# Linear attention and MLP, two layers: M as three float32r products, late parts of q behind it, and a new order in the first tile

## The chip, the cores and the metric

The kernel runs on one core of a Trainium2 chip. The time is the device time of one execution in microseconds, the median of several runs. Lower is better. A profile of one execution gives what each engine did: TensorE (PE, its weight loads PEld), VectorE (DVE), ScalarE (ACT), GpSimd (POOL) and SyncE (SP, which here issues transfers). "fp32r" is the type in which TensorE multiplies float32 data with one pass; the kernel gets its accuracy back by splitting an operand into a high part (rounded to fp32r) and a low part (the residual), and adding three products: high·high, low·high, high·low.

## The reference

Two layers, each with two halves, over x of 2048 rows and 640 columns; 32 heads of 20 columns:

```python
q, k, v = split(layernorm(x) @ wqkv)          # per head, S x 20
pq, pk = phi(q), phi(k)                       # where(t>0, t+1, exp(t)) + 1e-6
kv = einsum("bhsd,bhse->bhde", pk, v)         # 20 x 20 for each head
z  = einsum("bhsd->bhd", pk)
o  = (pq @ kv) / (pq . z + 1e-6)
x  = x + o @ wo                               # half A
h  = relu(layernorm(x) @ w1 + b1) ** 2
x  = x + h @ w2 + b2                          # half B
```

The kernel never forms v. With xh the normed rows, it accumulates G = xhᵀ·phi(k) over all rows, then kv = Gᵀ·wv restricted to the heads' diagonal blocks (a mask), and then M = kv·wo, a 640 x 640 matrix. So half A's output is (phi(q) divided by its denominator) @ M.

## The kernel before

All rows are cut into 16 tiles of 128. The instructions are laid out by hand: each engine runs them in the order in which the code issues them, and the 8 PSUM banks are assigned by number. SP issues transfers in order too.

**Half A, tile by tile.** A tile is normed, transposed (xT, high and low), and multiplied with the split weights kq into k and q (`part`, line 419 in the profile, three products for each of five blocks of 128). ACT takes the exponential from PSUM (`Phi.exp`, L519), DVE does the rest of phi (`Phi.rest`, L526 and L527). k goes to kh (high on ACT, low on DVE), POOL adds it to acc for the denominators (L727), and TensorE adds to G, whose five blocks stay in banks 3 to 7 (`g_part`). Columns 512 to 639 of phi(k) go to GT by `gt_part`, summed into SBUF by DVE (L557). q is stored to DRAM. For some tiles, those in LATE, q is not computed there: its halves of 320 columns wait as late parts, 15 matmuls each (`late_q`), to be run where TensorE would stand still.

**The first tile of layer 0** has an order of its own (L569 to L601 and L766). The weights arrive as raw blocks; ACT copies each to its high part (`first_loads.high`, L205), DVE makes the residual (`first_loads.low`, L211). ACT copies the transposed x out of two PSUM banks to xT's high part (L587), DVE makes its low part (L591). ACT's order before: high parts of the first and the second weight block, then the two copies of xT. TensorE then runs products 0 and 1 of each block and, LAG = 2 blocks later, product 2 (`first_part`).

**The stage around M**, once a layer, after the last tile. In the order of the code: late parts beside the split of acc and the denominators zbc; the last tile's G blocks, copied out of PSUM by ACT (L920); the last GT sums (L557); one late part (`late_q(1)`); five transposes of GT into banks 1 and 2 and their copy Gs (L929); the split of tile 0's divided q, pT (`b_split`, L148 and L149). Then six times `kv_make`: five (or ten) float32 matmuls (L957) into one of the banks 3 to 7 and 2, and DVE's multiplication by the mask into kvbd (L961). Between them DVE runs steps of tile 1's division (`b_step`, L651 to L672), spread by KV_STEPS. Then six times `m_make`, in the order M_ORDER: two float32 matmuls of 320 columns, kvbd by wo (L970), into two banks, from which ACT copies to Mc (L977) and stores it to DRAM; the last two blocks are also copied directly to Mr (L993). SP reads the stored rows in another arrangement into Mr (L999, `m_read`). Then four late parts (three by `late_q(Q[0])`, one more), the splits of Mr into uM (`m_split`, L1028 and L1029), and the projection `proj` of the first tiles (L440). Lists like `side_work` hold small moves of DVE that are run at given points.

wo comes into SBUF in the last tiles of half A by `load_vo`, on SP, as raw float32 rows. The rows of x for the residual sum of tiles 0 and 1 (`b_load_x`) are loaded within the loop over `kv_make`.

**Half B** (L1182, L1200 to L1205, L1242) is the MLP, with prepared weights; the change leaves it alone.

Of the kernel before, what the change touches and what calls it, by code (L numbers as in the profile page):

```python
# [65 lines left out]
OUT0 = (fast(4), fast(9))  # L66
STAY = 1
FB0 = 0
KV_STEPS = (0, 1, 1, 1, 1, 0)


M_ORDER = (0, 1, 2, 3, 5, 4)
# [18 lines left out]
def kernel(  # L91
# [382 lines left out]
    for layer in range(N_LAYERS):  # L474
        src = [rows(t, xf) for t in range(NT)] if layer == 0 else x2
        last_layer = layer == N_LAYERS - 1

        md = dram.tile([D, D], F32, name=f"md_{layer}", tag="md")
        pqd = [dram.tile([P, D], F32, name=f"pq_{layer}_{t}", tag=f"pq_{t}") for t in range(NT)]
# [79 lines left out]
        if layer == 0:  # L559

            psw = bank(3)

            def warm(n):
                for _ in range(n):
                    nc.tensor.transpose(psw[:, :P], ident, ident)

            warm(N_WARM)
            a_load(0, src)
            first_loads.step(0, 5)  # L569
            a_load(1, src)  # L570
            a_stats(0, add=nc.vector)
            first_loads.high(2)

            mv, rs = sts.pop(("a", 0))
            T4[0] = tmp.tile([P, TG, 2, D], R32, tag="T", name="xT", bufs=2)
            xT[0] = chunks(T4[0][:, 0])
            runs = [(bank(4), 0, 2), (bank(5), 2, DC)]
            for ps, a, b in runs:
                v = xt[0][:, a * P : b * P]
                nc.vector.tensor_scalar(v, v, mv[:, 0:1], rs, op0=ALU.subtract, op1=ALU.mult)  # L580
            for ps, a, b in runs:
                for c in range(a, b):
                    nc.tensor.transpose(
                        ps[:, (c - a) * P : (c - a + 1) * P], xt[0][:, c * P : (c + 1) * P], ident
                    )
                d = T4[0][:, 0, 0, a * P : b * P]
                nc.scalar.activation(d, ps[:, : (b - a) * P], AF.Copy)  # L587
            first_loads.low(1)
            for ps, a, b in runs:
                d = T4[0][:, 0, :, a * P : b * P]  # L590
                nc.vector.tensor_tensor(  # L591
                    out=d[:, 1], in0=ps[:, : (b - a) * P], in1=d[:, 0].bitcast(F32), op=ALU.subtract
                )
            first_loads.low(1)
            first_loads.step(2, 5)
            a_stats(1)
            first_loads.step(2, 5)
            a_apply(1)
            a_load(2, src)
            first_loads.step(1, 5)  # L600
            first_loads.high(1)  # L601
            first_loads.low(1)
# [15 lines left out]

        def load_vo(i):

            u = utile("uraw").bitcast(F32).rearrange("p (j n) -> p j n", j=2)
            for j in range(2):
                c = 2 * (i % 3) + j
                if i < 3 and c < DC:
                    nc.sync.dma_start(u[:, j], wqkv[c * P : (c + 1) * P, 2 * D :])
                if i >= 3:
                    n = head_rows(c)
                    nc.sync.dma_start(u[:n, j], wo[c * HR : c * HR + n, :])
                vo["v" if i < 3 else "o", c] = u[:, j]

        pq, xr, pT, yzp, yzx, xn = {}, {}, {}, {}, {}, {}
        dens, xTb = {}, {}
# [59 lines left out]
        def b_out(t, ps):  # L692
            proj(ps, pT.pop(t), M)
# [48 lines left out]
        for t in range(NT):  # L742
# [5 lines left out]
            if layer == 0:  # L748
                prep.store()
                if 6 <= t < 6 + 2 * DC:  # L750
                    keep_kq(*divmod(t - 6, 2))
            if t >= 13:
                b_load_pq(t - 13)
                load_vo(2 * t - 26)
                load_vo(2 * t - 25)
            if first:
# [15 lines left out]
                seq = [(nm, c) for nm in "kq" for c in range(DC)]  # L772
                for n in range(len(seq) + LAG):
                    if n < len(seq):
                        first_part(*seq[n], (0, 1))
                    if n >= LAG:
                        first_part(*seq[n - LAG], (2,))
                    if n == DC + LAG - 1:
                        for j in range(2):
                            fk.exp(j * HD, pss["k"][j][:, :HD])  # L780
                    if n == AT_T:
                        first_loads.high(2)
                        a_trans(1, bank(4, 2))
# [137 lines left out]
        for j in range(2):  # L921
            gt_part(NT // 2 - 1, j, xbank())
        b_blocks(0)
        late_q(1)

        psT = bank(1, 2)
        transpose5(psT, GT_)
# [12 lines left out]

        b_split(0, xtile("pT"))

        u = xtile("kvbd", F32).rearrange("p j n -> p (j n)")
        kvbd = [u[:, HR * c : HR * (c + 1)] for c in range(NH)]
        maskf = mask.rearrange("p h d -> p (h d)")
        kvb = [3, 4, 5, 6, 7, 2]

        def kv_make(c):
            n = head_rows(c)
            kvb.append(kvb.pop(0))  # L950
            ps = bank(kvb[-1])

            o, m = HR * c, max(min(DM - HR * c, n), 0)
            parts = [v for v in ((0, m, G, o), (m, n, Gs, max(o - DM, 0))) if v[0] < v[1]]
            for q0, q1, g, w0 in parts:
                for d in range(DC):
                    nc.tensor.matmul(  # L957
                        ps[:n, q0:q1], vo["v", d][:, o : o + n],
                        g[:, d, w0 : w0 + q1 - q0], start=d == 0, stop=d == DC - 1,
                    )  # L960
            nc.vector.tensor_tensor(out=kvbd[c][:n, :n], in0=ps[:n, :n], in1=maskf[:n, :n], op=ALU.mult)  # L961

        mb = [4, 2, 6]

        def m_make(c):
            mb.append(mb.pop(0))
            ps = bank(mb[-1], 2)
            n, o = head_rows(c), HR * c
            for j in range(2):
                nc.tensor.matmul(  # L970
                    ps[:n, j * 512 : j * 512 + HD], kvbd[c][:n, :n],
                    vo["o", c][:n, j * HD : (j + 1) * HD], start=True, stop=True,
                )

            if c not in M_NEAR:
                u = ftile("Mc")
# [56 lines left out]
        for c in range(NH):  # L1033
            kv_make(c)
            if c == 0:
                b_load_pq(3)
            if c == 1:
                b_load_x(0)
            if c == 3:
                b_load_x(1)  # L1040
            if KV_STEPS[c]:
                b_step(1, KV_STEPS[c])
        side_work.append(lambda: b_split(1, xtile("pT")))
        run_side(1)
        sg.close()
        sm = ExitStack()
        mp = sm.enter_context(
# [8 lines left out]
        for i, c in enumerate(M_ORDER):  # L1056
            m_make(c)
            b_step(2)
            for r in M_READ.get(c, ()):
                m_read(*r)  # L1060
            if i > 4:
                run_side(1)
            if i > 0:
                b_step(3)
        side_work.append(lambda: b_split(3, xtile("pT")))
        late_q(Q[0])
        for m in range(3):
            m_split(m)
        run_side(1)
        late_q(1)  # L1070
        m_split(3)
        m_split(4)
        m_sum(4)
# [604 lines left out]
```

## Time and profile before

| | before |
|---|---|
| median of 3 runs | 1342.88 us (1342.48 to 1343.03) |
| the profiled execution | 1345.11 us |
| its span in the trace | 1343.2 us |
| PE busy | 1336.0 us, 99% |
| DVE busy | 891.5 us, 66% |
| ACT busy | 697.8 us, 52% |
| POOL busy | 124.2 us, 9% |

The profiled execution is 2.2 us longer than the median, and its span covers all but 1.9 us of it. In the rows of a timeline stand the start (us from the span's start), the busy time, engine, line, operation, output and inputs, shapes, and the number of instructions that the row puts together; in square brackets stands the time the engine was idle before, and what released it. In rows of groups three durations stand as shortest, median and longest in ns, then the first and the last start.

### The profile page before, as it was taken

What the parts mean: (1) busy time and instruction counts of PE and PEld (TensorE: products, weight loads), DVE (VectorE), ACT (ScalarE), POOL (GpSimd) and SP (SyncE); (2) the same over time, 40 slices, a digit from 0 to 9 for tenths busy, and PEclk for the clock granted to TensorE, in tenths of its full rate; (3) what the DMA queues carried; (4) which work ended last, traced back from release to release, by engine and by line L of the source; (5) the groups of instructions that cost most, each with busy time, mean ns of one, the idle gap of its engine ahead of it and who ended that gap; (6) DMA issues with size and microseconds to landing.
All of it is one profiled execution on the core that took longest, in us unless ns stands there. A gap on an engine that the chain in (4) does not pass through costs nothing.

```text
span 1343.2 us, 18730 instructions
## 1 busy us (share of the span) xinstructions
PE 1336.0 (99%) x6746; PEld 1154.6 (86%) x6746; DVE 891.5 (66%) x1601; ACT 697.8 (52%) x1612; POOL 124.2 (9%) x171
## 2 busy tenths in 40 slices
PE   9999999999999999999999999999999999999998
PEld 8888999988888888888888899998888888888887
DVE  7888868877766756533367678678777567665323
ACT  4887844634545426424547686355434535454131
POOL 2222310000000000000012132100000000000000
PEclk9999999999999999999999999999999999999999
DMA  6787846575557475588521115176547565564654
GB/s 206 246 293 263 284 125 197 176 282 172 189 207 225 137 265 175 168 296 300 207 99 44 55 40 145 52 243 253 159 150 277 161 204 189 206 221 139 247 169 154
DMA packets 100638, 255.88 MB, mean 191 GB/s; under 512 B 12787, under 2 KB 37747, under 8 KB 99907
## 3 DMA queue, kind: packets, MB, share of 16 engines
q1 hardware_dynamic: 99322, 252.04, 55.6%
q10 hardware_dynamic: 1224, 2.65, 0.7%
q8 instruction: 53, 0.87, 0.3%
q14 instruction: 39, 0.31, 0.1%
HBM read 195.96 MB, written 58.49 MB: 189 GB/s over the span
## 4 chain that ended last, share of the span: by engine, by line
PE 99%; DMA 0%; ACT 0%; SPq 0%; DVE 0%; DVEq 0%; issue 0%
PE PS L419 38%; PE PS L1242 28%; PE PS L1182 28%; PE PS L440 3%; PE PS L970 1%; PE PS L957 1%; PE PS L766 1%; DMA st<-in_A_wqkv_dram 0%; PE PS L388 0%; PE PS L907 0%; PE PS L1282 0%; ACT kq L205 0%; DVE x L1293 0%; SPq L227 0%; SPq L457 0%; DVEq L1673 0%
## 5 line engine op out<-in xcount | busy, mean ns | idle before, releaser
L1182 PE MATMUL PS<-xTb,u 128*128 128x512 f32 x1400 | 332.8, 390 | 0.0
L407 ACT ACTIVATE z<-y 32x160 f32<-32x160 f32 x880 | 294.0, 334 | 59.3 <-DVE y L394 49.4
L1182 PEld LDWEIGHTS PS<-xTb,u 128*128 128x128 f32 x1400 | 262.4, 188 | 53.6
L419 PE MATMUL PS<-kq,xT 128*128 128x320 f32 (+2 forms) x1575 | 283.4, 335 | 0.0
L1242 PE MATMUL PS<-u,h 128*128 128x512 f32 x1120 | 279.6, 390 | 0.0
L419 PEld LDWEIGHTS PS<-kq,xT 128*128 128x128 f32 x1575 | 250.3, 188 | 26.7 <-DVE rl L527 0.5
L1200 ACT ACTIVATE hr<-PS,b1sb 128x512 f32<-128x512 f32 x104 | 71.4, 687 | 348.3 <-PE PS L1182 346.9
L1242 PEld LDWEIGHTS PS<-u,h 128*128 128x128 f32 x1120 | 208.1, 188 | 39.5
L1204 DVE TENSOR_TENSOR hr<-hr 128x512 f32<-128x512 f32 x104 | 71.3, 685 | 148.2 <-ACT h L1201 148.2
L419 PE MATMUL PS<-kh,xh 128*128 128x512 f32 x480 | 124.2, 392 | 0.0
L519 ACT ACTIVATE e<-PS 128x320 f32<-128x320 f32 (+4 forms) x128 | 53.4, 435 | 108.7 <-PE PS L419 99.1
L378 POOL TENSOR_SCALAR rs<-mv 128x1 f32<-128x1 f32 x63 | 28.8, 458 | 860.4 <-DVE mv L376 860.4
L419 PEld LDWEIGHTS PS<-kh,xh 128*128 128x128 f32 x480 | 87.2, 188 | 15.2 <-DVE kh L730 0.4
L526 DVE TENSOR_SCALAR e<-e 128x320 f32<-128x320 f32 (+4 forms) x128 | 41.6, 325 | 66.3 <-ACT e L519 66.3
L1242 PE MATMUL PS<-h,u 128*128 128x512 f32 x280 | 79.1, 391 | 0.0
L1205 DVE TENSOR_TENSOR h<-hr,h 128x512 fp32r<-128x512 f32 x104 | 72.0, 692 | 7.5
L727 POOL TENSOR_TENSOR acc<-acc,r 128x640 f32<-128x640 f32 x30 | 53.9, 1798 | 197.7 <-DVE r L527 197.7
L1201 ACT ACTIVATE h<-hr 128x512 fp32r<-128x512 f32 x104 | 65.8, 633 | 3.3
L1242 PEld LDWEIGHTS PS<-h,u 128*128 128x128 f32 x280 | 52.0, 188 | 10.5 <-DVE h L1218 0.4
L1450 DVE TENSOR_TENSOR xr<-PS,xr 128x320 f32<-128x320 f32 x48 | 23.5, 489 | 51.5 <-PE PS L419 50.2
L1182 PE MATMUL PS<-xTb,uw 128*128 128x512 f32 x240 | 57.0, 390 | 0.0
L527 DVE SCALAR_TENSOR_TENSOR r<-PS,e 128x512 f32<-128x512 f32 (+2 forms) x104 | 51.1, 492 | 5.8 <-ACT e L519 2.3
(136 smaller groups left out, 1551.2 us busy)
## 6 DMA issues: line engine op xcount, KB each, us to landing
u<-kept_w SPq DMA_DIRECT2D x184, 640.0 KB, 4.9
x<-x SPq DMA_DIRECT2D x48, 320.0 KB, 5.4
kept_w<-uprep SPq DMA_DIRECT2D x23, 640.0 KB, 5.2
pqt<-pq SPq DMA_DIRECT2D x128, 80.0 KB, 4.3
x<-xr SPq DMA_DIRECT2D x32, 320.0 KB, 2.4
st<-in_B_w_dram SPq DMA_DIRECT2D x22, 320.0 KB, 4.1
pq<-r SPq DMA_DIRECT2D x20, 320.0 KB, 2.3
kept_kq<-kq SPq DMA_DIRECT2D x10, 640.0 KB, 6.1
```

The source lines that it names most:

```text
L407: nc.scalar.activation(d, v, AF.Copy)
L419: nc.tensor.matmul(ps, a, b, start=first and i == 0, stop=last and i == 2)
L519: nc.scalar.activation(self.e[:, a:b], ps, AF.Exp)
L526: nc.vector.tensor_scalar(e, e, 1.0, PHI_EPS, op0=ALU.min, op1=ALU.add)
L527: nc.vector.scalar_tensor_tensor(out=self.r[:, a:b], in0=ps, scalar=0.0, in1=e, op0=ALU.max, op1=ALU.add)
L727: nc.gpsimd.tensor_tensor(out=acc, in0=acc, in1=r, op=ALU.add)
L1182: nc.tensor.matmul(ps, a[:, d, :], bb[:, d, :], start=n == 0, stop=n == len(order) - 1)
L1200: nc.scalar.activation(r, ps, AF.Relu, bias=b1sb[:, c : c + 1])
L1201: nc.scalar.activation(h[:, 0], r, AF.Square)
L1204: nc.vector.tensor_tensor(out=r, in0=r, in1=r, op=ALU.mult)
L1205: nc.vector.tensor_tensor(out=h[:, 1], in0=r, in1=h[:, 0].bitcast(F32), op=ALU.subtract)
L1242: nc.tensor.matmul(ps, l, r, start=first and k == 0, stop=last and k == len(a) - 1)
```

## The change

Three parts, all within half A.

1. **M as three fp32r products.** The six blocks of wo are split: ACT copies the high parts (`wo_high`) after the copies of G, POOL subtracts to get the low parts in place (`wo_low`). The masked kv goes to a float32 tile kvr, ACT copies its high part, and DVE makes the low part one block later (`kv_low`). `m_make` then runs six fp32r matmuls a block in place of two float32 ones. To be allowed as fp32r operands, the rows of wo are copied once within DRAM (`wod`, at tile 8 of layer 0) and loaded from there into fp32r tiles. Tile 1's division is run as a whole behind `kv_low`, and its split among the M blocks.
2. **Late parts.** The one between the GT sums and the transposes is gone; behind M now stand five, with banks 0, 1, 7, 2 and 3 in turn. Bank 7 is one that the last M block uses. The rests of phi for them are put off until the first splits of Mr are issued. The loads of x for tiles 0 and 1 are issued behind M's blocks. Two side moves after the projection change places with a residual sum.
3. **First tile.** ACT's order is now: the first weight's high part, the two copies of xT, the second weight's high part. DVE's residuals keep their order. TensorE runs all three products of the first block at once, and product 2 of the others as before.

```diff
-KV_STEPS = (0, 1, 1, 1, 1, 0)
...
+        if layer == 0:
+            wod = dram.tile([D, D], F32, name="wod", tag="wod")
...
-            first_loads.high(2)
+            first_loads.high(1)
...
             first_loads.low(1)
+            first_loads.high(1)
             for ps, a, b in runs:
...
-            u = utile("uraw").bitcast(F32).rearrange("p (j n) -> p j n", j=2)
+            w = utile("uraw").rearrange("p (j n) -> p j n", j=2)
+            u = w.bitcast(F32)
...
-                    nc.sync.dma_start(u[:n, j], wo[c * HR : c * HR + n, :])
-                vo["v" if i < 3 else "o", c] = u[:, j]
+                    nc.sync.dma_start(u[:n, j], wod[c * HR : c * HR + n])
+                vo["v" if i < 3 else "o", c] = u[:, j] if i < 3 else w[:, j]
...
+            if layer == 0 and t == 8:
+                nc.sync.dma_start(wod, wo)
...
-                        first_part(*seq[n], (0, 1))
-                    if n >= LAG:
+                        first_part(*seq[n], (0, 1, 2) if n == 0 else (0, 1))
+                    if n > LAG:
                         first_part(*seq[n - LAG], (2,))
...
         b_blocks(0)
-        late_q(1)
+        wo_hi = {}
+        def wo_high(i):
...
+            for c in (2 * i, 2 * i + 1):
+                n = head_rows(c)
+                nc.scalar.activation(wo_hi[c][:n], vo["o", c][:n].bitcast(F32), AF.Copy)
+        def wo_low(c):
+            n, v = head_rows(c), vo["o", c]
+            nc.gpsimd.tensor_tensor(
+                out=v[:n], in0=v[:n].bitcast(F32), in1=wo_hi[c][:n].bitcast(F32), op=ALU.subtract
+            )
+        for i in range(3):
+            wo_high(i)
+        for c in range(NH):
+            wo_low(c)
...
-            nc.vector.tensor_tensor(out=kvbd[c][:n, :n], in0=ps[:n, :n], in1=maskf[:n, :n], op=ALU.mult)
+            v = kvr[:n, kvc[c]]
+            nc.vector.tensor_tensor(out=v, in0=ps[:n, :n], in1=maskf[:n, :n], op=ALU.mult)
+            nc.scalar.activation(kvs[:n, 0, kvc[c]], v, AF.Copy)
+        def kv_low(c):
+            n = head_rows(c)
+            nc.vector.tensor_tensor(
+                out=kvs[:n, 1, kvc[c]], in0=kvr[:n, kvc[c]], in1=kvs[:n, 0, kvc[c]].bitcast(F32),
+                op=ALU.subtract,
+            )
...
-            for j in range(2):
-                nc.tensor.matmul(
-                    ps[:n, j * 512 : j * 512 + HD], kvbd[c][:n, :n],
-                    vo["o", c][:n, j * HD : (j + 1) * HD], start=True, stop=True,
-                )
+            w = wo_hi[c], vo["o", c]
+            for i, (k, l) in enumerate(((0, 0), (1, 0), (0, 1))):
+                for j in range(2):
+                    nc.tensor.matmul(
+                        ps[:n, j * 512 : j * 512 + HD], kvs[:n, k, kvc[c]],
+                        w[l][:n, j * HD : (j + 1) * HD], start=i == 0, stop=i == 2,
+                    )
...
-            if c == 1:
-                b_load_x(0)
-            if c == 3:
-                b_load_x(1)
-            if KV_STEPS[c]:
-                b_step(1, KV_STEPS[c])
+            if c > 0:
+                kv_low(c - 1)
+        kv_low(NH - 1)
+        b_step(1, 9)
         side_work.append(lambda: b_split(1, xtile("pT")))
-        run_side(1)
...
-            if i > 4:
+            if i > 3:
                 run_side(1)
...
-        late_q(Q[0])
-        for m in range(3):
-            m_split(m)
+        b_load_x(0)
+        b_load_x(1)
+        late_q(2, False)
+        xbanks = [7]
+        late_q(1, False)
+        m_split(0)
+        m_split(1)
+        xbanks = [2, 3, 0, 1]
+        late_q(1, False)
+        m_split(2)
+        late_q(1, False)
+        late_todo.insert(0, late_todo.pop(2))
+        late_rest()
         run_side(1)
-        late_q(1)
         m_split(3)
...
+            b_x1(i, po[i])
             run_side(2)
-            b_x1(i, po[i])
```

More of the change, by code (lines that the diff above doesn't have):

```diff
@@ L923 @@
         b_blocks(0)
-        late_q(1)
+        wo_hi = {}
+        def wo_high(i):
+            n = head_rows(2 * i + 1)
+            if i < 2:
+                v = xtile("uo")
+                wo_hi[2 * i], wo_hi[2 * i + 1] = v[:, 0], v[:, 1]
+            else:
+                wo_hi[4], wo_hi[5] = (ap.tile([P, D], F32, tag="r", name="uo", bufs=3).bitcast(R32) for _ in range(2))
+            for c in (2 * i, 2 * i + 1):
[10 more added lines that the diff above has]
+            wo_low(c)
         psT = bank(1, 2)
@@ L941 @@
         b_split(0, xtile("pT"))
-        u = xtile("kvbd", F32).rearrange("p j n -> p (j n)")
-        kvbd = [u[:, HR * c : HR * (c + 1)] for c in range(NH)]
+        kvr, kvs = ftile("kvr"), xtile("kvbd")
+        kvc = [slice(HR * c, HR * c + head_rows(c)) for c in range(NH)]
         maskf = mask.rearrange("p h d -> p (h d)")
```

## The prediction

> **What bounds the kernel now.** I read the page first: busy shares, then the chain that ended last.
>
> ```profile
> span 1343.2 us, 18730 instructions
> ...
> PE 1336.0 (99%) x6746; PEld 1154.6 (86%) x6746; DVE 891.5 (66%) x1601; ACT 697.8 (52%) x1612; POOL 124.2 (9%) x171
> ...
> PE 99%; DMA 0%; ACT 0%; SPq 0%; DVE 0%; DVEq 0%; issue 0%
> PE PS L419 38%; PE PS L1242 28%; PE PS L1182 28%; PE PS L440 3%; PE PS L970 1%; PE PS L957 1%; PE PS L766 1%; DMA st<-in_A_wqkv_dram 0%; PE PS L388 0%; PE PS L907 0%; PE PS L1282 0%; ACT kq L205 0%; DVE x L1293 0%; SPq L227 0%; SPq L457 0%; DVEq L1673 0%
> ```
>
> TensorE is the bound, 99% of the span. So an edit is worth what it does to the PE stream: matmul time that goes, and idle time that comes. The page cannot say more; the change touches three short stretches, and I read those in the timeline: the first tile of layer 0, and the stage between the end of G and the projection, once in each layer (layer 1 repeats it 663 us later).
>
> First tile, from the chain, the timeline and the windows (columns of a window: PE, PEld, DVE, ACT, POOL busy, granted PE clock, DMA share, GB/s):
>
> ```profile
> 1.69 5.77 DMA st<-in_A_wqkv_dram
> ...
> 7.48 0.74 ACT kq L205
> 8.22 0.28 ACT xT L587
> ...
> 6.18 0.94 PE L583 MATMUL PS<-ident,xt 128*128 128x128 f32 x5 [0.29 <-DVE xt L580]
> 8.12 0.75 ACT L587 ACTIVATE xT<-PS 128x256 fp32r<-128x256 f32 x2
> 8.54 8.26 PE L766 MATMUL PS<-kq,xT 128*128 128x320 f32 x44 [1.42 <-ACT xT L587]
> 11.61 2.41 ACT L205 ACTIVATE kq<-st 128x640 fp32r<-128x640 f32 x3 [0.86 <-DMA st<-in_A_wqkv_dram]
> ...
> 5.26:8.67 3.41, 1.69 (x12) 1.03 (x11) 1.69 (x4) 1.19 (x4) 0.42 (x1) 1.00 0.95 337
> 8.67:12.09 3.42, 3.42 (x13) 3.37 (x14) 3.42 (x7) 2.56 (x5) 0.00 (x0) 0.50 1.04 401
> 20.00:30.00 10.00, 10.00 (x55) 8.39 (x53) 9.76 (x22) 4.38 (x9) 2.28 (x5) 1.00 0.33 96
> ```
>
> The transposes of x end at 7.12, but their copies stand on ACT behind the second weight's copy, which waits for its transfer until 7.48. PE idles 1.42 us. After a window in which PE worked half the time (1.69 of 3.41 us) the granted clock is 0.50 for one window.
>
> The stage around M in layer 0:
>
> ```profile
> 195.88 2.64 ACT L920 ACTIVATE G<-PS 128x512 f32<-128x512 f32 x4
> 199.48 2.37 PE L419 MATMUL PS<-kq,xT 128*128 128x320 f32 x15
> 199.68 0.49 DVE L557 TENSOR_TENSOR GT<-PS,GT 128x320 f32<-128x320 f32 x1 [0.39 <-PE PS L419]
> 200.69 0.83 DVE L667 TENSOR_TENSOR pqt<-pqt,den 128x640 f32<-128x640 f32 x1
> 201.68 0.71 PE L388 MATMUL PS<-ident,GT 128*128 128x128 f32 x5
> 202.23 5.34 PE L957 MATMUL PS<-G,uraw 128*120 128x120 f32 x50
> 203.03 0.73 ACT L148 ACTIVATE pT<-z 128x640 fp32r<-128x640 f32 x1
> 203.79 0.83 DVE L149 TENSOR_TENSOR pT<-z,pT 128x640 fp32r<-128x640 f32 x1 [0.58 <-ACT pT L148]
> 205.64 0.28 DVE L961 TENSOR_TENSOR kvbd<-PS,mask 120x120 f32<-120x120 f32 x1
> 209.09 7.03 PE L970 MATMUL PS<-uraw,kvbd 120*120 120x320 f32 x24
> 210.47 0.70 ACT L977 ACTIVATE Mc<-PS 120x640 f32<-120x640 f32 x1
> 214.29 0.70 ACT L977 ACTIVATE Mc<-PS 120x640 f32<-120x640 f32 x1 [0.45 <-DVE den L665]
> 215.72 9.21 PE L419 MATMUL PS<-kq,xT 128*128 128x320 f32 x60
> 216.17 2.85 ACT L993 ACTIVATE Mr<-PS 32x640 f32<-32x640 f32 x4
> 223.10 1.98 ACT L1028 ACTIVATE uM<-Mr 128x640 fp32r<-128x640 f32 x3
> 224.77 1.48 PE L440 MATMUL PS<-uM,pT 128*128 128x320 f32 x9
> ```
>
> PE is never idle here: one late part of q (199.48) lies over VectorE's sums of GT, kv follows at 202.23, M at 209.09, four late parts at 215.72, the projection at 224.77. M takes 6.63 us of PE by these starts (215.72 − 209.09), 0.276 a matmul. The late parts take 9.05 us for 60 matmuls, 0.15 each. The late parts cover M's way out: copies, stores, reads, and uM at 223.10.
>
> **The change, part by part.**
>
> *First tile.* The copies of xT now stand on ACT ahead of the second weight's copy. The first can follow the second transpose, at about 6.6, and PE's products start near 7.1 rather than 8.54: 1.4 us earlier. PE's window to 8.67 is then busy for 1.7 + 1.5 = 3.2 of 3.4 us, so the half clock after it, which stretches 13 matmuls over 3.42 us, may not come. Against that: weights land at the transfers' pace (a share of 1.04 in that window, and ACT still waits for them before 11.61), and VectorE is busy 9.76 of 10 us from 20 to 30, so it can take some of the gain back. Bounds: 0 if the weights or VectorE set the end, 2.5 if the half-clock window goes too. I take 1.4 gained, the idle time that the row shows. The third pass at n = 0 only moves PE work.
>
> *Late part removed ahead of the transposes.* PE loses 15 × 0.15 = 2.2 us, and the cover of the GT sums with it: the second sum ends at 199.68 + 0.49 = 200.17, the two transposes of the first half may run before it, the other three after, so PE gets to kv at 200.6, idle for some 0.6. Gain 202.23 − 200.6 = 1.6.
>
> *M in three products.* 36 matmuls of 320 columns × 0.15 = 5.4 us in place of 6.63: 1.3 gained. It needs new operands, and here is the price:
> - six copies of wo on ACT (0.73 each by the pT row, about 0.63 apart) from the end of G (195.88 + 2.64, then one more copy: 198.5). They end near 202.3, ahead of Gs and pT, which had begun at 202.4 and 203.0; Gs is needed only by kv's last blocks. Nothing.
> - six copies of kv's high part on ACT, about 0.3 each (an estimate from the mask's 0.28 on the same tile), and they stand ahead of the first Mc.
> - six masks as before and six residuals of kv on VectorE, about 0.28 each; tile 1's division (b_step) is put behind them. The split of tile 1's pT had its copy at 209.8 and is wanted after the first tile's projection, beyond 227, so that move costs nothing.
> - six residuals of wo on POOL, 120 x 640. Their nearest rows are these:
>
> ```profile
> L727 POOL TENSOR_TENSOR acc<-acc,r x30: 1613/1628/2089, 32.5 to 850.5; 128x640 f32<-128x640 f32 x30
> ...
> L149 DVE TENSOR_TENSOR xh<-xt,xh x32: 815/1602/1618, 25.7 to 850.3; 128x640 fp32r<-128x640 f32 x32
> L149 DVE TENSOR_TENSOR pT<-z,pT x8: 817/826/826, 203.8 to 889.7; 128x640 fp32r<-128x640 f32 x8
> ...
> 187.12 0.82 DVE L149 TENSOR_TENSOR xh<-xt,xh 128x640 fp32r<-128x640 f32 x1
> 187.35 2.02 POOL L727 TENSOR_TENSOR acc<-acc,r 128x640 f32<-128x640 f32 x1 [6.77 <-DVE r L527]
> 188.01 2.04 DVE L730 TENSOR_TENSOR kh<-r,kh 128x640 fp32r<-128x640 f32 x1
> ```
>
> Each takes 1.62 us, so six are 9.8 us from 199.3 to at least 209. The rows show more: the same subtraction on VectorE takes 0.82 where POOL rests (pT), and 1.60 by the median where POOL adds to acc (xh). At 187 one sees the order: VectorE's first ends at 187.94, POOL's takes until 189.37, VectorE's next, begun at 188.01, ends at 190.05. They run one after another, never together. In this stage POOL rested; now it works just when VectorE has two-input work: L667, pT's residual, and the new residuals of kv.
>
> So two sums. Mc's first copy starts at X, and X follows the last high copy of kv. Before, from X = 210.47, the last Mr copy ended 8.55 us later (216.17 + 2.85). Now pT of tile 1 falls between: 9.1. The third late part is put in bank 7, which M's last block fills, so it waits for those Mr copies, and three parts (6.6 us) stand from there to the projection: projection = X + 15.7. Before it was X + 14.3. No loss needs X = 209.07 or less.
> - If POOL and VectorE do not hinder each other: kv ends 207.45, X = 208.5, projection at 224.2: 0.6 gained a layer. (By PE alone: 1.6 + 1.3 gained, 2.2 for the fifth part, the same 0.7; the bank 7 wait is then 0.1.)
> - If they alternate: POOL 199.3 to 200.9, L667 behind POOL's second at 202.6, pT's residual behind the fourth, at 206.4, kv's first residual 208.6, its second 210.3, when POOL is through; masks 2 to 5 stand between the residuals on VectorE, so the last high copy ends at 211.8 = X. Projection at 227.5, 2.7 later a layer. PE waits some 3 us within M and again ahead of the third part.
>
> I take the second, because the rows of just these instruction kinds show it and there is no row where they ran together. "SBUF — State Buffer" of the Trainium skill, section "Who interferes with whom", gives the rule: VectorE and GpSimd share a port pair as an exclusive lock, which a VectorE instruction with two SBUF inputs takes against a GpSimd instruction that reads SBUF, and the loser fully blocks. The rows at 187 agree (2.04 for 0.82), so by this rule too the change pays the second sum.
>
> *The rest.* wo is copied once inside DRAM at tile 8 of layer 0 (1.6 MB on SP's queue) and read from there; the share of the DMA engines in the windows after the first tile is 0.33, and wo is wanted at 198: nothing, unless SP's stores behind it are late by a few us, which no row shows. The residual input of tiles 0 and 1 is loaded behind M's reads on SP: wanted only when a tile's projection ends, past 229. The deferred rests of phi stand behind uM's residuals on VectorE. Side moves and the first residual change places after the projection has begun. Each nothing while PE has the projection's matmuls to run.
>
> **Sum.** 2 × 2.7 − 1.4 = +4.0 us. The profiled execution took 1345.1 us (1.9 around its span), 2.2 more than the median; the difference is taken against the median: 1342.9 + 4.0 = 1346.9.
>
> **Rivals.**
> 1. *No hindrance* (faster side): the residuals of wo end before VectorE needs the port, or 120-partition work passes. Decided by X at or under 208.4. For: masks take one input from PSUM and need no second port; PE's sum is a gain. Against: the xh row. 2 × (−0.6) − 1.4 = −2.6: 1340.3; with 2.5 in the first tile 1339.2, below the limit of measurement (0.2%, 2.7 us, is about what can be told from no change).
> 2. *Half hindrance*: VectorE gets ahead of POOL at each turn, as at 187.12, and kv's residuals lose two turns rather than four: X near 210, +0.9 a layer, 2 × 0.9 − 1.4 = +0.4: 1343.3.
> 3. *Hindrance, and the clock falls*: PE, some half busy between 207.5 and 211, gets 0.50 for one 3.4 us window, as after 5.26 to 8.67. The work of half a window is lost, 1.7 us, where PE and not ACT sets the pace: +1 a layer on the sum, 1348.9. "TensorE: Matmul & The Clock Gate" of the skill, section "What's actually happening", says that one idle window of about 3.4 us halves the clock. The row at 8.67 agrees with 0.50, though its window was half busy and not idle.
> 4. *The first part does nothing*: the weights' transfers set the end of the first tile; 1.4 more on any case.
>
> **How the numbers follow.** Hindrance, rivals 3 and 4 on it included: 0.52, of which 0.10 ends within 0.2% (X below 211.1, where the total is +2.7). Half hindrance 0.2: 0.16 within, 0.03 faster, 0.01 slower. No hindrance 0.28: it stands on the limit, and as the two gains by PE can be larger than I count (the bank 7 wait gone, the half-clock window gone), I give 0.24 of it to faster, 0.04 to no change. So faster 0.27, same 0.3, slower 0.43. The range goes from 1339.0 (rival 1, with the larger first tile) to 1349.5 (rival 3 with part of rival 4); about 0.1 lies on either side; the likeliest case's own is 1345 to 1349.
>
> **What would show it.** First tile: the products start near 7.1, and the row of 0.50 clock shrinks. Hindrance: residuals of kv or L667 with over 1 us on VectorE, POOL's six at 1.6 to 2.1, first Mc at 211 to 212, and idle time of PE before the third late part released by ACT's Mr. Rival 1: kv's residuals at 0.3 and the first Mc near 208.5, with the projection near 224.2 less the first tile's gain. I am wrong if POOL's subtractions run beside VectorE's, or if another row (a transfer of wo, SP) holds PE.

## The result, and the profile after

The changed kernel takes 1347.59 us (five runs, 1346.89 to 1351.22) against 1343.03 us before (1342.48 to 1343.18): 1.0039 times as long, 95% interval 1.0028 to 1.005. It is 4.6 us slower; 4.0 was forecast (1346.9). The difference is small, 0.4%, and clear of the scatter of the runs. The profiled execution is the median one, 1347.59 us, with a span of 1345.8.

The page of the changed kernel, its busy times and its chain:

```profile
span 1345.8 us, 18849 instructions
...
PE 1334.4 (99%) x6770; PEld 1156.1 (86%) x6770; DVE 903.6 (67%) x1613; ACT 708.9 (53%) x1636; POOL 144.8 (11%) x183
...
PE 96%; DVE 3%; DMA 1%; ACT 0%; SPq 0%; issue 0%; POOL 0%; DVEq 0%; ACTq 0%
```

PE is still busy 99% of the span, but the chain that ended last now runs 3% through VectorE, where it had none. The stage around M in layer 0 follows, in the timeline. Line numbers are those of the changed kernel: L671 is the former L667, L148 the split's residual, L946 wo's residual on POOL, L992 the mask, L997 kv's residual, L1011 M, L1018 Mc, L1034 Mr, and L387, L418 and L439 are the former L388, L419 and L440. Each run below has numbers of its own, a few lines off.

```profile
196.76 1.92 PE L418 MATMUL PS<-xh,kh 128*128 128x320 f32 x12
198.26 10.28 POOL L946 TENSOR_TENSOR uraw<-uraw,uo 120x640 fp32r<-120x640 f32 x6 [9.87 <-ACT uo L942]
199.27 0.55 PE L387 MATMUL PS<-ident,GT 128*128 128x128 f32 x3 [0.37 <-DVE GT L559]
199.65 5.34 PE L987 MATMUL PS<-G,uraw 128*120 128x120 f32 x50
200.27 1.73 DVE L671 TENSOR_TENSOR pqt<-pqt,den 128x640 f32<-128x640 f32 x1
203.69 1.90 DVE L148 TENSOR_TENSOR pT<-z,pT 128x640 fp32r<-128x640 f32 x1 [0.80 <-ACT pT L147]
206.21 0.92 DVE L997 TENSOR_TENSOR kvbd<-kvr,kvbd 120x120 fp32r<-120x120 f32 x1 [0.24 <-ACT kvbd L993]
206.52 0.41 PE L1011 MATMUL PS<-uo,kvbd 120*120 120x320 f32 x1
207.25 1.43 DVE L997 TENSOR_TENSOR kvbd<-kvr,kvbd 120x120 fp32r<-120x120 f32 x1
207.38 0.70 PE L1011 MATMUL PS<-uo,kvbd 120*120 120x320 f32 x3 [0.45 <-DVE kvr L992]
208.80 0.27 DVE L997 TENSOR_TENSOR kvbd<-kvr,kvbd 120x120 fp32r<-120x120 f32 x1
209.77 0.82 PE L1011 MATMUL PS<-uo,kvbd 120*120 120x320 f32 x4 [1.40 <-DVE kvr L992]
209.80 0.68 ACT L1018 ACTIVATE Mc<-PS 120x640 f32<-120x640 f32 x1
214.57 11.20 PE L418 MATMUL PS<-kq,xT 128*128 128x320 f32 x75
216.01 2.85 ACT L1034 ACTIVATE Mr<-PS 32x640 f32<-32x640 f32 x4
225.60 6.61 PE L439 MATMUL PS<-uM,pT 128*128 128x320 f32 x44
```

The reader is to see POOL's row from 198.26 to 208.54, and below it the four VectorE instructions with two SBUF inputs that fall into it: 1.73, 1.90, 0.92 and 1.43 us. As soon as POOL is through, the next residual of kv takes 0.27. PE waits 0.45 and 1.40 us within M for masks that stand behind those residuals on VectorE.

Taken one by one, POOL's six show the other side of it. They took 1.55, 1.55, 2.13, 1.53, 2.12 and 1.59 us; the rows of the second, the third and the fifth:

```profile
199.77 1.55 POOL L946 TENSOR_TENSOR uraw<-uraw,uo 120x640 fp32r<-120x640 f32 x1
201.28 2.13 POOL L946 TENSOR_TENSOR uraw<-uraw,uo 120x640 fp32r<-120x640 f32 x1
204.87 2.12 POOL L946 TENSOR_TENSOR uraw<-uraw,uo 120x640 fp32r<-120x640 f32 x1
```

L671 starts at 200.27 and ends at 202.00, 0.68 us after POOL's second. The third starts while L671 is still to run, and takes 0.58 longer than the second; the fifth does the same beside pT's residual (203.69 to 205.59). So where both have such work, the two engines go in turn, and the one that comes second waits.

Layer 1 does the same again, and more. Its last products of GT and its projection in the timeline, and two windows within M (the seventh value is the granted clock):

```profile
861.20 1.92 PE L418 MATMUL PS<-xh,kh 128*128 128x320 f32 x12
891.54 1.63 PE L439 MATMUL PS<-uM,pT 128*128 128x320 f32 x10
...
871.32:874.73 3.41, 1.54 (x9) 1.26 (x9) 3.39 (x11) 1.53 (x5) 1.67 (x2) 1.00 0.00 0
874.73:878.14 3.41, 3.41 (x15) 3.41 (x14) 3.24 (x6) 1.61 (x3) 0.00 (x0) 0.50 0.56 137
```

The row of the same products before, in layer 0:

```profile
197.72 1.92 PE L419 MATMUL PS<-xh,kh 128*128 128x320 f32 x12
```

From the last GT products to the projection it takes 30.34 us in layer 1 (891.54 − 861.20), in layer 0 28.84 (225.60 − 196.76), before 27.05 (224.77 − 197.72). The 1.5 that layer 1 takes more than layer 0 come with a granted clock of 0.50 from 874.73 to 878.14, behind a window in which PE was busy for 1.54 of 3.41 us.

### The profile page after: what moved, and what is told of

Same layout as the page of the kernel before. It is cut to its first block, busy times and chain, and to the rows that moved or that the text cites. A ratio compares the mean times of both kernels' runs of the same rounds, so it can differ in the third digit from the quotient of the medians.

```text
span 1345.8 us, 18849 instructions
## 1 busy us (share of the span) xinstructions
PE 1334.4 (99%) x6770; PEld 1156.1 (86%) x6770; DVE 903.6 (67%) x1613; ACT 708.9 (53%) x1636; POOL 144.8 (11%) x183
## 4 chain that ended last, share of the span: by engine, by line
PE 96%; DVE 3%; DMA 1%; ACT 0%; SPq 0%; issue 0%; POOL 0%; DVEq 0%; ACTq 0%
PE PS L418 36%; PE PS L1289 28%; PE PS L1229 28%; PE PS L439 3%; PE PS L1011 1%; DMA st<-in_A_wqkv_dram 1%; DVE kvbd L997 0%; DVE pT L148 0%; DVE e L528 0%; DVE r L529 0%; DVE pqt L671 0%; DVE bn L373 0%; PE PS L387 0%; SPq L226 0%; ACT kq L204 0%
## 5 line engine op out<-in xcount | busy, mean ns | idle before, releaser
L418 PE MATMUL PS<-kq,xT 128*128 128x320 f32 (+2 forms) x1575 | 282.3, 334 | 0.0
L418 PEld LDWEIGHTS PS<-kq,xT 128*128 128x128 f32 x1575 | 250.3, 188 | 25.2 <-DVE xT L148 0.2
L418 PE MATMUL PS<-kh,xh 128*128 128x512 f32 x480 | 124.1, 392 | 0.9 <-DVE kh L734 0.8
L418 PEld LDWEIGHTS PS<-kh,xh 128*128 128x128 f32 x480 | 87.2, 188 | 16.0 <-DVE kh L734 1.2
```

The costliest lines, as they stand in the source:

```text
L418: nc.tensor.matmul(ps, a, b, start=first and i == 0, stop=last and i == 2)
```

## The experiments

All times stand beside runs of the kernel before on the same chip: 1342.83 us in the first group (no_low, set_low, first_only, early_dve), 1342.95 in the second (before_again, no_first, early_nofirst, late_kept), 1342.96 in the third (f32_late, early_pool, best, first_acc). In brackets stand the ratio to before and its 95% interval. A difference between kernels of different groups, or from the 1347.59 above, is one between medians of different sets of runs.

**Does POOL's reading block VectorE?** Three theories: A, POOL and VectorE block each other; B, the new chain is longer by its own work; C, POOL is merely late. Two edits of the changed kernel, each by itself (`REPS` is 3):

```diff
-        for c in range(NH):
-            wo_low(c)
```

> POOL's six subtractions are left out, so the third product multiplies kv's high part with the whole wo instead of its residual, and nothing else is changed. Theory A (POOL and VectorE block each other): kv's residuals take 0.3 us instead of 0.9 and 1.4, L671 and pT's residual 0.8 instead of 1.7 and 1.9, the first Mc copy in layer 0 comes about 2 us earlier (near 207.8 instead of 209.8), and no idle time over 0.6 us stays within M; 4 to 6 us less than the changed kernel, so 1341.5 to 1343.5. Theory B (the chain is longer by its own copies, masks and residuals, whatever POOL does): 1347 to 1348, the same. Theory C (POOL's results are merely late for the third product): at most 1 us less, 1346.5, as the rows show PE waiting for masks and high copies and not for POOL.

```diff
         def wo_low(c):
...
-            nc.gpsimd.tensor_tensor(
-                out=v[:n], in0=v[:n].bitcast(F32), in1=wo_hi[c][:n].bitcast(F32), op=ALU.subtract
-            )
+            for _ in range(REPS):
+                nc.gpsimd.memset(v[:n].bitcast(F32), 0.0)
```

> In place of each of POOL's subtractions stand three fills with zero of the same 120 x 640 block, so POOL is busy at the same place but reads nothing (the residual of wo is zero here). Theory A, with reading as what matters: the same as without POOL's work as far as VectorE goes, two-input instructions at 0.3 and 0.8 us, 1341.5 to 1344, the upper end if the fills end late. Theory A, with any POOL access blocking: as the changed kernel, 1346 to 1348.5. Theory C: as the changed kernel if the fills end as late as the subtractions (208.5 in layer 0).

Measured: 1341.31 us without POOL's work, 1341.23 us with the fills. Both are 6.3 to 6.4 less than the changed kernel and 1.5 to 1.6 less than before (both 0.9989, 0.998 to 0.9998). The rows of the kernel with fills, in the timeline and the group of kv's residuals:

```profile
197.41 11.76 POOL L948 MEMSET uraw<- 120x640 f32 x18 [9.85 <-ACT uo L943]
198.30 0.47 DVE L669 TENSOR_SCALAR den<-den 128x32 f32<-128x32 f32 x1
199.19 0.83 DVE L672 TENSOR_TENSOR pqt<-pqt,den 128x640 f32<-128x640 f32 x1
201.73 0.82 DVE L149 TENSOR_TENSOR pT<-z,pT 128x640 fp32r<-128x640 f32 x1 [0.83 <-ACT pT L148]
206.87 0.70 ACT L1018 ACTIVATE Mc<-PS 120x640 f32<-120x640 f32 x1 [0.61 <-PE PS L1011]
...
L997 DVE TENSOR_TENSOR kvbd<-kvr,kvbd x12: 191/279/285, 203.2 to 868.7; 120x120 fp32r<-120x120 f32 x10, 40x40 fp32r<-40x40 f32 x2
```

POOL is busy longer than with the subtractions (11.76 against 10.28 us) and at the same place, and yet the same VectorE instructions are back at 0.83, 0.82 and 0.28 us. So it is not POOL's time nor its lateness but its reading of SBUF. B falls, since the chain's own copies, masks and residuals are all there; C falls, since the fills end 13.2 us after the GT products (209.17 − 195.93) and the subtractions ended after 11.8. Of the 6.3 us a part is the clock, as the kernel no_first below shows. "SBUF — State Buffer" of the Trainium skill, section "Who interferes with whom", says that a GpSimd instruction that only writes does not contend with a VectorE instruction of two SBUF inputs; these rows agree.

**The residuals elsewhere.** The high copies go to ACT's idle time ahead of the late parts, the residuals to VectorE's; `wo_low` now calls `nc.vector.tensor_tensor`, and its old calls behind G are gone:

```diff
+        for i in range(3):
+            wo_high(i)
+        for c in range(2):
+            wo_low(c)
         late_q(1)
         ah = xtile("ah")
         split(ah[:, 0], ah[:, 1], acc)
+        wo_low(2)
         late_q(1)
...
         b_den(0)
+        wo_low(3)
...
+        wo_low(5)
+        wo_low(4)
         b_blocks(0)
```

> The changed kernel with wo's high copies on ACT ahead of the first late part (about 188 in layer 0), and its residuals on VectorE: two before the late parts, one behind acc's split, one behind tile 0's denominators, two behind the GT sums. POOL does nothing in the stage. Theory A: VectorE pays 6 x 0.82 = 4.9 us, mostly in its idle time between 190 and 199; the first Mc copy near 207.8, no idle time over 0.6 us within M, projection 0.6 us earlier a layer than before besides the first tile's 1.0: 1340.8, and 1340 to 1343. Theory B: 1346 to 1348.

Measured 1341.44 us (0.999, 0.9981 to 1.0). This bears out theory A again, 0.6 above the number. The same kernel with the first tile's order as before:

> wo's high copies early on ACT and its residuals on VectorE, with the first tile's order as before. Adding up: 1341.4 - 1.3 = 1340.2, 2.6 us less than before. If the first tile's part is worth nothing by itself: 1341.4.

Measured 1341.37 us (0.9989, 0.998 to 0.9997), so the first tile's part is worth nothing here, and the parts do not add up. The same place, with the first tile as before, but with POOL in place of VectorE for the residuals:

> wo's high copies early on ACT as in the two early kernels, but the residuals on POOL, right behind its last addition to acc (189.4 to 199 in layer 0), first tile as before. VectorE has gaps there, so blocking costs less than behind G: the residual of acc and tile 0's denominators pay up to 1.6 us each, and PE waits up to 1.4 us for acc's split; kv's residuals are free. 2 x 1.0 above the early kernel: 1343.4. If POOL's reading costs wherever VectorE works: 1345 or more. If the gaps take it all: 1341.4.

Measured 1344.50 us (1.001, 1.0002 to 1.0019), 3.1 more than with VectorE. Its timeline:

```profile
186.93 11.10 POOL L919 TENSOR_TENSOR uraw<-uraw,uo 120x640 fp32r<-120x640 f32 x6
191.25 1.65 DVE L148 TENSOR_TENSOR ah<-acc,ah 128x640 fp32r<-128x640 f32 x1
192.82 1.68 DVE L528 TENSOR_SCALAR e<-e 128x320 f32<-128x320 f32 x1
192.95 0.85 PE L935 MATMUL PS<-ah,ones 128*128 128x320 f32 x4 [1.69 <-DVE ah L148]
```

The six cost 1.69 us of PE a layer by the blocked split of acc, at a place where VectorE had gaps (in the changed kernel it is busy for 9.03 of 14 us from 185 to 199). In the stage's own place they cost 6.3 in all, the clock included (1347.59 − 1341.31). So the blocking moves with the reads, and what it costs is set by what stands behind the blocked instruction.

**The late part.** First the changed kernel with the late part back ahead of the transposes, then the kernel before with the late move alone:

```diff
         for c in range(NH):
             wo_low(c)
+        late_q(1)
...
         late_q(2, False)
-        xbanks = [7]
-        late_q(1, False)
         m_split(0)
...
-        late_todo.insert(0, late_todo.pop(2))
```

> The changed kernel with the late part of q back ahead of the GT transposes and four behind M, none in bank 7; POOL's subtractions as in the changed kernel. VectorE is as late as before, since POOL sets it, while kv ends 1.6 us later: so PE waits less within M (some 1.6 less of its 3 us), but the fifth part no longer stands behind M. If POOL's blocking sets the first Mc copy (209.8 in layer 0), the projection comes at that time + 9.1 + the rest of M's way out, near 224.6, about 1 us a layer earlier than in the changed kernel: 1345.5. If the late move itself was a gain of 0.7 a layer: 1349.

Measured 1343.21 us (1.0002, 0.9993 to 1.001): 4.4 less than the changed kernel and level with before, though POOL's subtractions are all there. Its timeline:

```profile
195.79 1.92 PE L418 MATMUL PS<-xh,kh 128*128 128x320 f32 x12
197.29 10.40 POOL L946 TENSOR_TENSOR uraw<-uraw,uo 120x640 fp32r<-120x640 f32 x6 [9.86 <-ACT uo L942]
208.93 0.82 PE L1012 MATMUL PS<-uo,kvbd 120*120 120x320 f32 x4 [0.64 <-DVE kvr L993]
222.51 6.05 PE L439 MATMUL PS<-uM,pT 128*128 128x320 f32 x40
229.10 3.21 PE L439 MATMUL PS<-uM,pT 128*128 128x320 f32 x20 [0.54 <-DVE uM L1071]
```

kv comes 1.6 us later and so hides most of the blocking: one wait of 0.64 is left within M, and the projection comes 26.72 us after the GT products, 0.3 sooner than before; 0.54 is lost behind it. I had forecast 1 us a layer. Against the changed kernel's layer 0 it is 2.1 at the projection, and 1.2 by the GT products of layer 1 (from GT products to GT products 663.20 us here, 664.44 in the changed kernel). Its profiled execution also has no half-clock window, which took 1.5 in the changed kernel's. So most of what the blocking costs is paid because the late part was taken from in front of it. Some is paid even so: the kernel is 1.9 above the one without POOL's work, though that one differs in the late part too.

> The kernel before with the second part alone: no late part ahead of the GT transposes, five behind M, M as before in float32, first tile as before. PE loses its cover of the GT sums (an idle time of 0.5 a layer in the changed kernel's rows) and keeps the same matmuls; M's last copies end before the third late part, so bank 7 does not wait: 2 x 0.5 = 1.0 us slower, 1343.9. If the fifth part behind M were a gain by itself (M's way out was late): 1342.5 or less.

The edit is the two hunks on the late parts and the loads of x, on the kernel before; the first residual sum (`b_x1`) stays behind its side moves. Measured 1344.71 us (1.0013, 1.0004 to 1.0022), 1.75 slower than before. Its timeline:

```profile
197.37 0.55 PE L388 MATMUL PS<-ident,GT 128*128 128x128 f32 x3 [0.36 <-DVE GT L557]
243.06 3.21 PE L419 MATMUL PS<-kq,xT 128*128 128x320 f32 x20 [0.51 <-DVE xr L697]
```

PE waits 0.36 a layer for the GT sums, and 0.51 at a place that I had not listed: a late part behind the projection waits for VectorE's L697, the residual sum `b_x1`, which stands behind the side moves here. 2 x (0.36 + 0.51) = 1.74 is as much as the loss between the medians, though the traces show more: from the GT products of layer 0 to those of layer 1 the kernel takes 1.2 us more than before (859.30 − 194.86 against 859.05 − 195.81), so the two idle times are not all of it. In the changed kernel `b_x1` stands ahead of the side moves, and this wait is not there. That suggests that the exchange, costed at nothing, is worth about 1 us where the rests are put off (an estimate from the two waits of 0.51; no run has the exchange alone). The late move gains nothing by itself.

**The first tile.** A second profile of the kernel before, the new order alone, that order with POOL's addition for tile 1 moved, and the changed kernel without it:

> The kernel before once more, unchanged, for a second profile. The profiled execution of before was 2.2 us over the median and had a window of 0.50 clock in the first tile; the first tile's new order alone came out 1.3 us slower than the median. If other executions have no such window, this profile shows the clock at 1.00 up to 36 us, the tile-1 products of q ending 1.5 to 2.3 us earlier than in the first profile, and a time near 1342.8. If it has the window again at 1345, the loss of the new order lies behind the first tile.

This one run took 1343.31 us. The first tile of this second execution, in the timeline and its window, and then the rows at the last products of GT and at the projection of both layers:

```profile
6.55 0.74 ACT L205 ACTIVATE kq<-st 128x640 fp32r<-128x640 f32 x1 [1.21 <-DMA st<-in_A_wqkv_dram]
7.62 7.26 PE L766 MATMUL PS<-kq,xT 128*128 128x320 f32 x44 [0.41 <-ACT xT L587]
14.72 0.71 PE L388 MATMUL PS<-ident,xt 128*128 128x128 f32 x5
...
8.67:12.09 3.42, 3.31 (x23) 3.04 (x22) 3.38 (x7) 2.09 (x4) 0.22 (x1) 1.00 1.04 407
...
195.81 1.92 PE L419 MATMUL PS<-xh,kh 128*128 128x320 f32 x12
222.85 9.40 PE L440 MATMUL PS<-uM,pT 128*128 128x320 f32 x63
859.05 1.92 PE L419 MATMUL PS<-xh,kh 128*128 128x320 f32 x12
886.09 7.20 PE L440 MATMUL PS<-uM,pT 128*128 128x320 f32 x48
```

The second weight's copy began 0.9 us earlier than in the first profile, PE waited 0.41 instead of 1.42, and the clock stayed at 1.00. The second tile's transposes came at 14.72, in the first profile at 16.64, and this difference of 1.9 is still there at the projection of layer 1 (886.09; 887.94 in the first). So the first profile was over the median by what happened in its first tile, and the idle time on which I had put 1.4 us belongs to that execution. Such times are rare: of the 92 runs of the kernel before in the three groups, four took 1344.9 to 1345.4 us, all others 1342.1 to 1343.6.

> The kernel before with the first tile's new order alone. By the two traces the new order is 1.5 us ahead at the second tile's transposes (15.13 against 16.64), and 0.55 of it is lost by 46 us, where VectorE was late by 0.8 (35.85): 1342.0, 1.0 less than before. Rival: the gain is a matter of the half-clock window's position in each run, then 1341 to 1343.5 with more spread than before.

Measured 1344.09 us (1.001, 1.0001 to 1.0019), 1.26 slower than before, where 1.0 faster was expected. Its timeline:

```profile
14.68 0.71 PE L388 MATMUL PS<-ident,xt 128*128 128x128 f32 x5
30.51 1.58 POOL L728 TENSOR_TENSOR acc<-acc,r 128x640 f32<-128x640 f32 x1 [2.11 <-DVE r L527]
30.57 1.73 DVE L526 TENSOR_SCALAR e<-e 128x384 f32<-128x384 f32 x1
35.41 1.66 PE L419 MATMUL PS<-kh,xh 128*128 128x512 f32 x6 [0.83 <-DVE kh L731]
```

The second tile's transposes come at 14.68 against 14.72, so ACT's order gains nothing by then; that the weights' transfers set the end of the first tile fits this, for ACT waits for one of them in either order (0.86 us ahead of 11.61 in the first profile of before, 0.92 ahead of 11.60 in the changed kernel). And POOL's addition to acc now starts just ahead of VectorE's 128 x 384 instruction, which takes 1.73 us; 4 us later PE waits 0.83. To see whether that is the loss, the addition is moved:

```diff
-            else:
+            elif t > 1 or layer > 0:
                 nc.gpsimd.tensor_tensor(out=acc, in0=acc, in1=r, op=ALU.add)
             for f in between:
                 f()
+            if t == 1 and layer == 0:
+                nc.gpsimd.tensor_tensor(out=acc, in0=acc, in1=r, op=ALU.add)
```

> The first tile's new order alone, with POOL's addition of tile 1 to acc put behind the statistics of tile 4 on POOL, so that it no longer blocks VectorE's 128 x 384 instruction (1.73 us instead of 0.35 at 30.57) ahead of the products that waited 0.83. If that wait is the loss: 1344.1 - 0.8 = 1343.3. If the loss is elsewhere: 1344.1.

Measured 1342.61 us (0.9997, 0.9989 to 1.0006), 1.5 less than the new order alone and level with before. The 128 x 384 instruction takes 0.36 us there, and PE's wait is gone: the same mechanism as in the stage around M. But it accounts for a part of the 1.5 only. The last row of matmuls begins at 1334.12 in the trace of the new order alone and at 1333.16 here, 0.96 apart, while the spans end 1.8 apart (1342.4; 1340.6): the rest lies behind the last matmul, and why is open. In the early kernel on VectorE, which has the new order too, the same instruction takes 1.70 us and PE waits 0.78, and yet the median is no worse than with the old order.

> The changed kernel with the first tile's order as before. The first tile's part alone cost 1.26 us, so if the parts add up: 1347.6 - 1.3 = 1346.3. If the first tile's loss was a matter of that kernel alone: 1347.6.

Measured 1346.68 us (1.0036, 1.0024 to 1.0047), with runs from 1344.59 to 1352.58. Between single runs the granted clock is the difference: 1.000 from 1344.59 to 1345.80, 0.998 or 0.999 at 1346.6 to 1346.7, 0.995 at 1350.2 and 1350.8, 0.993 at 1352.58. The kernels without the blocking and the kernel before stay within 2.5 us of their median, at 0.998 to 1.000. So at the full clock the blocking costs some 3.2 to 4.4 us (1344.59 to 1345.80 against 1341.37 for the early kernel on VectorE with the same first tile), and the rest is the clock. In the changed kernel's layer 1 PE's idle time within M was thus paid twice: in itself, and by the half-clock window behind it. Where the clock fell in the other runs is not seen, since one execution of each kernel is profiled.

**A kernel that is faster than both.** This is the early kernel on VectorE with the first tile as before, the last products of GT ahead of the last two of G, and the late part in bank 7 as the last of the five. The edit for GT:

```diff
         for i in range(DC):
+            if i >= DC - 2:
+                gt_part(NT // 2 - 1, i - DC + 2, xbank())
             g_part(NT - 1, i)
             nc.scalar.activation(G[:, i], bank(GB[i]), AF.Copy)
-        for j in range(2):
-            gt_part(NT // 2 - 1, j, xbank())
```

> The early kernel on VectorE, first tile as before, and two more changes: the two last products of GT stand ahead of the two last of G, so G's products cover the GT sums (0.5 a layer), and the late part in bank 7 is the last of the five instead of the third (the five took 11.34 us a layer there, 11.03 in the changed kernel: 0.3). 1341.4 - 2 x 0.8 = 1339.8, 3.1 less than before.

Measured 1340.17 us (0.998, 0.9971 to 0.9989), 2.8 less than before. Its timeline:

```profile
197.70 0.71 PE L387 MATMUL PS<-ident,GT 128*128 128x128 f32 x5
205.11 0.85 PE L1013 MATMUL PS<-uo,kvbd 120*120 120x320 f32 x4
210.81 11.15 PE L418 MATMUL PS<-kq,xT 128*128 128x320 f32 x75
221.80 10.38 PE L439 MATMUL PS<-uM,pT 128*128 128x320 f32 x67
```

The transposes run without the 0.37 of idle time, the five late parts take 10.99 us, and M in three products takes 5.70 (210.81 − 205.11) in place of 6.63. So the three products gain 0.9 us a layer, once their operands are made where nothing waits for them.

## Why the prediction was right, and where it was not

The time was within the range, on the side that was forecast, 0.7 us from the number, and the mechanism that was forecast, POOL and VectorE in turn, is the one that the runs show. But that the sum came so close is luck. Against the second profile of before, which has no disturbance in the first tile, the changed kernel is late by 0.95 us at the GT products of layer 0 (196.76 against 195.81), by 2.75 at the projection (225.60; 222.85), by 2.15 at the GT products of layer 1 (861.20; 859.05), by 5.45 at its projection (891.54; 886.09) and by 4.88 from the MLP that follows to the last matmuls; behind these it gets 0.4 back (the spans end at 1345.8 and 1341.3). So the first tile costs 0.95, the stages 1.80 and 3.30, and 0.6 is given back behind each stage. The forecast had −1.4, +2.7 and +2.7; the trace has +0.95, +1.2 and +2.7, and 1.5 of the last is the clock.

- *First tile, 1.4 gained*: wrong, in sign too. The step that failed is to take the idle time that one row shows as the gain. PE's products did start early, at 7.01, but the second tile's transposes came at 15.13, no sooner than the 14.72 of before's second profile. That is rival 4, where the transfers set the end. A blocked VectorE instruction came on top: PE waits 0.81 for kh at 35.85. The whole costs 1.26 us alone, of which its trace shows 0.5 at the last matmuls; in the changed kernel's trace it is 0.95 by the GT products. Between the medians of the changed kernel with and without it stand 0.9, which the scatter of the latter (1344.59 to 1352.58) does not tell from nothing.
- *Late part ahead of the transposes, 1.6 gained at kv's begin, at the price of idle time*: right. From the GT products to kv 2.89 us against 2.88 in the forecast. What it took away was a cover for VectorE too, which I did not price; late_kept shows 2.1 us for it at layer 0's projection, 1.2 by the next layer.
- *M, 36 x 0.15 = 5.4*: 5.70 where nothing hinders it. Right but for 0.3: in early_nofirst and in best a weight load of the last block waits 0.26 for ACT's Mc copy. For the others the profile names no releaser.
- *Hindrance, X = 211.8*: the mechanism was right, the size too large. Counted from the GT products X came 13.04 us later, forecast 14.08, so 1.0 less. The order of turns is the forecast one: L671 behind POOL's second, pT's residual behind the fourth, kv's first two residuals behind the fifth and the sixth. The term mis-sized is the length of a turn: POOL's six took 10.28 us where I had 11.0 (199.3 to 210.3), 1.55 each where nothing holds them and not 1.62, and they gave way twice, by 0.6 each, where I had a whole VectorE instruction (0.82). X then came 1.26 us after POOL's end, where I had 1.5.
- *Projection = X + 15.7*: 15.80. The number is right, but by another path: the third late part began at about 218.98, two fifths into the 11.03 us from 214.57, and Mr's last copy ended at 218.86, so bank 7 was free just in time and PE's own work set the end. The wait for bank 7 shows where M is on time: the five take 11.34 us in early_nofirst, with a wait of 0.34 for ACT's Mr, and 10.99 in best.
- *2.7 a layer*: 1.80 in layer 0 and, with 1.5 of the clock, 3.30 in layer 1; 0.6 of each came back.
- *Rival 3, the clock falls*: it happened in layer 1 of the profiled execution (0.50 for 3.41 us, a loss of 1.5 where I had 1.7) and shows in the clocks of single runs. I had held it for a rival; it is a part of the result, and it fills the place of the size that was too large.
- *Rival 1, no hindrance, 1340.3*: the kernels without POOL's reads took 1341.2 to 1341.4. The forecast of what the change would be worth without the block was a microsecond too good, which the first tile's 1.4 would explain.
- *Rival 2, X near 210*: by before's count X was 210.8 (197.72 + 13.04), between its 210 and the forecast's 211.8.
- *The rest at nothing*: no row of the changed kernel contradicts it. But the exchange of side moves and residual sum seems to be what makes it true: f32_late, without it, waits 0.51 a layer. Neither the exchange, nor the copy of wo, nor the loads of x was tried by itself.

## What to carry to other kernels

Before work is put on an idle POOL, look at what VectorE does in those microseconds: an instruction with two inputs in SBUF, or a TENSOR_SCALAR from SBUF to SBUF, is stretched by what is left of POOL's (here 0.28 to 1.43 us and 0.35 to 1.73), and whatever stands behind it on VectorE is late too. Matmuls that cover a wait also cover the chain behind it: where they are taken out, that chain pays too, not the place alone where they stood. And an idle time that one profiled execution shows at a kernel's start, where transfers set the pace, is worth a second profile before it is counted as gain.

## What the runs showed of the hardware that I had not expected

When POOL and VectorE both have work queued, each can hold the other, and they go in turn: POOL's subtractions took 1.53 to 1.59 us where nothing held them and 2.13 and 2.12 behind a VectorE instruction that is 0.82 by itself; single VectorE instructions went from 0.28 to 1.43 us. POOL's instructions are the longer ones here, so VectorE lost more by it.

Fills by POOL leave a two-input instruction alone (0.82 and 0.83 us) but not every instruction: the TENSOR_SCALAR of 128 x 32 took 0.47 us beside them, 0.17 in the kernel without POOL's work.

And PE need not stand still for the clock to fall. After 1.69 of 3.41 us busy it was 0.50 in the first profile of before, after 1.54 in layer 1 of the changed kernel; after 2.88 in the second profile of before it stayed at 1.00. Layer 0 of the changed kernel has the same waits and no drop. Its busy time from 206.40 to 209.81 was 1.56 us, as little as in layer 1; but in steps of 3.413 us, the length of the slow window, counted back from 874.73, the waits fall into two windows, with 2.20 us busy from 205.72 and 2.78 from 209.13. So these rows fit a clock that is set by fixed windows, and then it is chance which layer pays; no run was made to test it.
